# Patch rows of a depthwise convolution laid out as (row, column) instead of (column, row) on the partitions

**Chip, cores, metric.** One core of a Trainium2 chip. The metric is the device time of one execution in microseconds (us); a run's time is the median of its executions.

## The reference

```python
x0 = x + sum over 3x3 of shifted(x) * dw_pe        # depthwise convolution, 511 x 511 x 192, bf16
h  = layernorm(x0)                                 # over the 192 channels
# windows of 7 x 7 (73 x 73 = 5329 of them), 4 heads of 48:
q, k, v = split(h_windows @ w_qkv)
out = softmax(q k^T / sqrt(48)) v @ w_o
return x0 + out
```

## The kernel before

Windows are taken in 42 blocks of 128. For each block the tile XP holds, for every window, the 9 x 9 patch of x around it: 81 partitions, one for each patch position, and (window, channel) along a partition. The convolution is a matmul for each channel: 81 patch positions against T, an 81 x 49 matrix of that channel's taps. XP has one buffer; it is refilled for the next block as soon as the last convolution matmul of this block has read it, and is wanted again some 87 us later.

```python
for j in range(3):                                    # taps, one column of the 3x3 at a time
    nc.sync.dma_start(out=dwK[9 * j : 9 * j + 3, :], in_=dw_pe[:, j, :])
...
def load_xp(blk):
    for (a, b0, b1, p0) in segments(blk):             # runs of windows in one row of windows: 2 or 3
        nb = b1 - b0
        if a == NWR - 1 and blk > 0:
            nc.gpsimd.memset(XP[0:KP, p0 : p0 + nb, :], 0.0)
        else:
            if b0 == 0:
                nc.gpsimd.memset(XP[0:9, p0 : p0 + 1, :], 0.0)            # L119
            if b1 == NWC:
                nc.gpsimd.memset(XP[64:KP, p0 + nb - 1 : p0 + nb, :], 0.0)  # L121
        ...
        for pc in range(9):                           # patch column
            ...                                       # q, sh, bb0, bb1: which column of which window
            nc.sync.dma_start(                        # L139: nine rows onto nine neighbouring partitions
                out=XP[9 * pc + pr0 : 9 * pc + pr1, p0 + bb0 - b0 : p0 + bb1 - b0, :],
                in_=xr[h0 + pr0 : h0 + pr1, bb0 + sh : bb1 + sh, q, :],
            )
...
def conv_tile(blk, it):
    ...
    nc.tensor.matmul(ps[:, col : col + S], lhsT=XP[0:KP, :, c], rhs=T[0:KP, c, :], ...)   # L282
    nc.vector.tensor_tensor(out=xc[...], in0=ps, in1=xc[...], op=ALU.add)                 # L284
```

The stores (L396, SP queue) write XC, the finished block, in pieces of 16 windows; the loads of the next XC (L108, POOL queue) follow piece by piece, and the convolution of the next block adds into it. L412 and L431 are the q, k and v projections, L453 to L560 the attention, L346 the transposes after the norm, L369 the output projection.

## Time and profile before

| | before |
|---|---|
| time, median of 2 | 5343.16 us (5342.79 to 5343.53) |
| span of the profiled run, mean granted PE clock | 5337.2 us, 0.824 |
| first convolution matmul | 109.8 us |
| XP burst of a block: packets, length | 10,330, 53.5 us (mean of blocks 1 to 40) |
| 40 blocks in the middle | 4976.4 us |

The burst lengths and the block times are not a view of the profile: I grouped the XP packets (384 B each) in the trace's packet records, and took a block from the first convolution matmul of one block to that of the next. The profile's wait lines read "who waited, for whom: us in total, times, longest". "issue" as the releaser means that the engine waited for nothing that the profile shows.

### The profile page before, as it was taken

What the parts mean: (1) busy time and instruction counts of PE and PEld (TensorE: products, weight loads), DVE (VectorE), ACT (ScalarE), POOL (GpSimd) and SP (SyncE); (2) the same over time, 40 slices, a digit from 0 to 9 for tenths busy, and PEclk for the clock granted to TensorE, in tenths of its full rate; (3) what the DMA queues carried; (4) which work ended last, traced back from release to release, by engine and by line L of the source; (5) the groups of instructions that cost most, each with busy time, mean ns of one, the idle gap of its engine ahead of it and who ended that gap; (6) DMA issues with size and microseconds to landing.
All of it is one profiled execution on the core that took longest, in us unless ns stands there. A gap on an engine that the chain in (4) does not pass through costs nothing.

```text
span 5337.2 us, 148265 instructions
## 1 busy us (share of the span) xinstructions
PE 4490.1 (84%) x65427; PEld 3661.5 (69%) x65427; DVE 3816.7 (72%) x6912; ACT 2744.5 (51%) x3385; POOL 758.0 (14%) x833
## 2 busy tenths in 40 slices
PE   2788888888888888888988888888888888888887
PEld 1666676667776676677776777767666776677776
DVE  6776777767776777777677777777777777767776
ACT  1554555545555555555555455555555555545555
POOL 1111111111111111111111111111111111111120
PEclk9887888887778887888788877788888888877888
DMA  6554445554455555554455544455555445544431
GB/s 67 51 75 70 68 71 80 82 73 68 68 68 70 71 72 74 71 74 71 68 73 91 75 68 68 68 72 72 74 72 72 73 70 78 85 74 67 68 48 32
DMA packets 512613, 375.27 MB, mean 70 GB/s; under 512 B 453129, under 2 KB 453321, under 8 KB 511958
## 3 DMA queue, kind: packets, MB, share of 16 engines
q1 hardware_dynamic: 480918, 265.08, 38.1%
q0 software_dynamic: 30592, 100.32, 10.6%
q8 instruction: 514, 8.42, 0.7%
q14 instruction: 141, 1.16, 0.1%
q10 hardware_dynamic: 448, 0.30, 0.0%
HBM read 265.31 MB, written 100.27 MB: 68 GB/s over the span
## 4 chain that ended last, share of the span: by engine, by line
PE 44%; DVE 16%; ACT 14%; DMA 12%; SPq 9%; issue 4%; POOL 1%; DVEq 0%; ACTq 0%; POOLq 0%
PE ps L412 12%; PE ps L282 8%; SPq L396 7%; DMA out_dram<-XC 7%; PE ps L369 6%; DMA XC<-in_x_dram 5%; PE ps L453 5%; PE ps L532 4%; DVE kT L424 4%; ACT hT L355 4%; DVE Qb L422 3%; PE ps L431 2%; DVE XC L284 2%; PE ps L560 2%; ACT kT L426 2%
## 5 line engine op out<-in xcount | busy, mean ns | idle before, releaser
L412 PE MATMUL ps<-hT,Wqk 96*128 96x392 bf16 x5336 | 1233.5, 380 | 76.7 <-DVE XC L284 62.2
L478 ACT ACTIVATE PT<-ps 128x784 bf16<-128x784 f32 x667 | 552.7, 829 | 1095.3 <-PE ps L453 1080.3
L421 ACT CAST Qb<-ps 64x784 bf16<-64x784 f32 x667 | 555.3, 833 | 657.5 <-PE ps L412 655.7
L412 PEld LDWEIGHTS <-Wqk 96*128 96x128 bf16 x5336 | 529.4, 108 | 486.1 <-issue 252.5
L284 DVE TENSOR_TENSOR XC<-ps,XC 128x980 bf16<-128x980 f32 x378 | 437.9, 1176 | 503.0 <-PE ps L282 247.2
L282 PE MATMUL ps<-T,XP 81*128 81x49 bf16 x8064 | 744.0, 264 | 55.5 <-DMA XP<-in_x_dram 55.5
L567 ACT CAST OT<-ps 96x784 bf16<-96x784 f32 x667 | 541.0, 811 | 456.0 <-PE ps L560 452.4
L282 PEld LDWEIGHTS <-XP 81*128 81x128 bf16 x8064 | 733.9, 220 | 57.6 <-issue 55.5
L431 PE MATMUL ps<-Wv,hT 96*128 96x192 bf16 x5336 | 663.5, 277 | 16.4 <-DVE On L544 9.0
L532 PE MATMUL ps<-V,PT 49*64 49x49 bf16 x21344 | 542.5, 195 | 159.1 <-DVE Qb L422 81.2
L431 PEld LDWEIGHTS <-hT 96*128 96x128 bf16 x5336 | 548.8, 111 | 180.0 <-issue 91.6
L544 DVE TENSOR_TENSOR On<-ps,rs 128x768 bf16<-128x768 f32 x667 | 634.6, 951 | 16.0
L532 PEld LDWEIGHTS <-PT 49*64 49x64 bf16 x21344 | 466.2, 116 | 260.4 <-issue 217.7
L327 POOL TENSOR_TENSOR D<-ident,rstd 128x896 bf16<-128x896 bf16 x294 | 486.2, 1681 | 1074.8 <-DVE rstd L320 1053.3
L424 DVE CAST kT<-ps 128x784 bf16<-128x784 f32 x462 | 450.0, 974 | 219.2 <-PE ps L412 209.1
L304 DVE BATCH_NORM_STATS2 bnst<-XC 128x6 f32<-128x192 bf16 x2058 | 600.5, 343 | 0.2
L453 PE MATMUL ps<-Qb,kT 128*64 128x98 bf16 x10672 | 408.0, 225 | 180.7 <-DVE Qb L422 132.2
L422 DVE CAST Qb<-ps 64x784 bf16<-64x784 f32 x462 | 451.6, 978 | 110.6 <-ACT Qb L421 100.1
L355 ACT CAST hT<-ps 96x896 bf16<-96x896 f32 x462 | 452.4, 1109 | 135.9 <-PE ps L346 134.9
L560 PE MATMUL ps<-ident,On 128*96 128x98 bf16 x5336 | 412.1, 226 | 114.4 <-DVE kT L424 110.9
L453 PEld LDWEIGHTS <-kT 128*64 128x64 bf16 x10672 | 341.5, 121 | 231.5 <-issue 131.7
L108 POOL DMA_DIRECT2D XC<-in_x_dram x386 | 216.0, 560 | 1865.9 <-DVE rs L543 996.3
(73 smaller groups left out, 4396.2 us busy)
## 6 DMA issues: line engine op xcount, KB each, us to landing
XC<-in_x_dram POOLq DMA_DIRECT2D x277, 294.0 KB, 7.5
out_dram<-XC SPq DMA_DIRECT2D x277, 294.0 KB
XP<-in_x_dram SPq DMA_DIRECT2D x210, 246.4 KB
XP<-in_x_dram SPq DMA_DIRECT2D x68, 243.0 KB
XC<-in_x_dram POOLq DMA_DIRECT2D x37, 165.4 KB, 7.1
out_dram<-XC SPq DMA_DIRECT2D x37, 165.4 KB
XP<-in_x_dram SPq DMA_DIRECT2D x22, 216.0 KB
XP<-in_x_dram SPq DMA_DIRECT2D x18, 212.6 KB
```

The costliest lines, as they stand in the source:

```text
L282: nc.tensor.matmul(ps[:, col : col + S], lhsT=XP[0:KP, :, c], rhs=T[0:KP, c, :], start=True, stop=True)
L304: nc.vector.bn_stats(out=bnst[:, s, :], in_=xc[:, s, :])
L355: nc.scalar.copy(out=hv[0:KT, kt, :, s0 : s0 + NDG], in_=src)
L412: nc.tensor.matmul(ps[:, ab * 512 : ab * 512 + TOK], lhsT=Wqk[kt][0:KT, which * 2 + ab, :], rhs=hT[0:KT, kt, ck * CH : (ck + 1) * CH, 0:S] ...
L421: nc.scalar.copy(out=dst[0:64, :, :, 0, :], in_=src[0:64])
L422: (nc.vector.tensor_copy if dve_help else nc.scalar.copy)(out=dst[64:128, :, :, 1, :], in_=src[64:128])
L424: nc.vector.tensor_copy(out=dst[:, :, 0:TOK], in_=two_bank(ps, TOK))
L431: nc.tensor.matmul(ps[:, col : col + C], lhsT=hT[0:KT, kt, ck * CH + 2 * jj : ck * CH + 2 * jj + 2, :].rearrange("p w s -> p (w s)"), rhs= ...
L453: nc.tensor.matmul(ps[64 * wp : 64 * wp + 64, col : col + 2 * S], lhsT=k_[:, ab, w * S : w * S + 64], rhs=q_[:, ab, w, :, :].rearrange("p ...
L478: nc.scalar.activation(out=pt[:, 0 : 16 * S].rearrange("p (b n) -> p b n", b=2), in_=two_bank(ps, 8 * S), func=ACTF.Exp, scale=scale,)
L532: nc.tensor.matmul(ps[64 * wp : 64 * wp + 64, col : col + S], lhsT=pt[64 * wp : 64 * wp + S, pc_ : pc_ + 64], rhs=v_[64 * wp : 64 * wp + S ...
L544: nc.vector.tensor_tensor(out=o_[:].rearrange("p (b j) (h d) -> p b (j h) d", b=2, d=DH), in0=ov[:, :, :, 0:DH], in1=r_[:].rearrange("p (b ...
```

## The change

The intent: the nine rows of one load should fall on partitions nine apart instead of on nine neighbours. That neighbours slow a load down was the author's assumption. The partition of a patch position becomes 9 x row + column. The taps and the selection pattern that builds T are transposed to match. The halo columns now lie nine partitions apart; the change loads them from a small zero tile where the kernel before used a memset.

```diff
-        nc.sync.dma_start(out=dwK[9 * j : 9 * j + 3, :], in_=dw_pe[:, j, :])
+        nc.sync.dma_start(out=dwK[9 * j : 9 * j + 3, :], in_=dw_pe[j])
...
+    zero = consts.tile([16, C], BF, name="zero")
+    nc.vector.memset(zero[:], 0.0)
+    XPr = XP[0:KP].rearrange("(r q) n c -> q r n c", q=9)
...
             if a == NWR - 1 and blk > 0:
-                nc.gpsimd.memset(XP[0:KP, p0 : p0 + nb, :], 0.0)
-            else:
-                if b0 == 0:
-                    nc.gpsimd.memset(XP[0:9, p0 : p0 + 1, :], 0.0)
-                if b1 == NWC:
-                    nc.gpsimd.memset(XP[64:KP, p0 + nb - 1 : p0 + nb, :], 0.0)
+                nc.gpsimd.memset(XP[64:KP, p0 : p0 + nb, :], 0.0)
+            if a == 0 and blk > 0:
+                nc.gpsimd.memset(XP[0:9, p0 : p0 + nb, :], 0.0)
...
+            if b0 == 0 and blk > 0:
+                nc.sync.dma_start(out=XPr[0, :, p0, :], in_=zero[0:9, :])
+            if b1 == NWC and blk > 0:
+                nc.sync.dma_start(out=XPr[8, :, p0 + nb - 1, :], in_=zero[0:9, :])
...
-                    out=XP[9 * pc + pr0 : 9 * pc + pr1, p0 + bb0 - b0 : p0 + bb1 - b0, :],
+                    out=XPr[pc, pr0:pr1, p0 + bb0 - b0 : p0 + bb1 - b0, :],
...
-        pattern=[[-1, WS], [-9, WS], [1, KP]],
+        pattern=[[-9, WS], [-1, WS], [1, KP]],
```

## The prediction

The sum came to 11 us, 7 from part 2 and 4 from part 5; part 1 counts 0. The 300 packets per us in part 2 are the author's estimate: the nearest rate in the trace of the kernel before is 290, in a block's tail (rival (a)).

> **What bounds the kernel now.** I read the head of the page first, then the chain that ended last, then the waits, then the timeline of one block, then the issue queue that carries the changed loads.
>
> The page: busy shares, DMA queues and chain.
>
> ```profile
> span 5337.2 us, 148265 instructions
> PE 4490.1 (84%) x65427; PEld 3661.5 (69%) x65427; DVE 3816.7 (72%) x6912; ACT 2744.5 (51%) x3385; POOL 758.0 (14%) x833
> ...
> q1 hardware_dynamic: 480918, 265.08, 38.1%
> q0 software_dynamic: 30592, 100.32, 10.6%
> ...
> PE 44%; DVE 16%; ACT 14%; DMA 12%; SPq 9%; issue 4%; POOL 1%; DVEq 0%; ACTq 0%; POOLq 0%
> PE ps L412 12%; PE ps L282 8%; SPq L396 7%; DMA out_dram<-XC 7%; PE ps L369 6%; DMA XC<-in_x_dram 5%; PE ps L453 5%; PE ps L532 4%; DVE kT L424 4%; ACT hT L355 4%; DVE Qb L422 3%; PE ps L431 2%; DVE XC L284 2%; PE ps L560 2%; ACT kT L426 2%
> ```
>
> PE is the densest engine and has the largest part of the chain. The DMA in the chain is the stores (out_dram from XC) and the loads of XC that follow them; the loads of XP, which the change touches, do not appear among the chain's lines, although they are most of queue q1's 480,918 packets. So: busy queue, not the path.
>
> The waits, all engines, the lines that touch XP, XC and the POOL queue:
>
> ```profile
> POOL XP L121 <- PE ps L282: 1525.0, 41, 70.7
> ...
> POOL XC L108 <- DMA out_dram<-XC: 499.1, 248, 33.1
> ...
> DVE XC L284 <- DMA XC<-in_x_dram: 215.9, 34, 10.5
> ...
> PE ps L282 <- DMA XP<-in_x_dram: 55.5, 1, 55.5
> ```
>
> The convolution (L282) waits for XP once in the whole run: at the start. In the other 41 blocks it never does. The 1525 us are POOL waiting to zero the halo of XP until PE has read the old block; POOL is 14% busy and its next work (D from rstd) comes later anyway, so this large number costs nothing by itself. The XC wait of DVE (216 us, 34 times) is the chain proj, store, load, conv; XP is not in it.
>
> One block in the timeline of the SP queue (start, us, instruction):
>
> ```profile
> 2100.62 50.49 SPq L139 DMA_DIRECT2D XP<-in_x_dram  x27
> 2171.47 14.76 SPq L396 DMA_DIRECT2D out_dram<-XC  x10
> ```
>
> Two stretches of the prologue with nothing else running (length, busy time of PE, weight load, DVE, ACT, POOL, then granted clock, DMA share, GB/s):
>
> ```profile
> 85.00:90.00 5.00, 0.00 (x0) 0.00 (x0) 0.00 (x0) 0.00 (x0) 0.00 (x0) 1.00 0.68 71
> 90.00:105.00 15.00, 0.00 (x0) 0.00 (x0) 0.00 (x0) 0.00 (x0) 0.00 (x0) 1.00 0.70 96
> ```
>
> The 27 XP loads of a block are issued in 50 us and done before the stores. From 85 to 105 us every engine is idle and only XP moves, at 71 to 96 GB/s: the prologue is the one place where XP sets the time.
>
> From the trace's packet records I counted the XP packets (384 B) of each block: about 10,330, in 53.5 us on average (44 to 62), so 193 per us or 74 GB/s. From the last packet to the next convolution 25 to 46 us pass (median 33), to the first store 3 us at the least and 11 in the median. Blocks repeat every 124 us.
>
> [...]
>
> [...]
>
> [...]from 40 to 45 us, XC packets (nearly all 5,376 B) start at 25 per us over 16 engines and XP packets at 11 per us[...].
>
> **The change part by part.** The instruction streams, with line and buffer numbers taken out, are identical on PE and ACT. The rest:
>
> 1. XP loads: same count, same 384 B rows, same sources. Only the partition step of the destination goes from 1 to 9. [...]On the path: none of it, as 25 us of slack exist already. Gain per block 0.
>
> 2. Prologue: the first convolution starts at 109.7 us, after 9,686 XP packets. Until about 80 us XP is held back by the XC loads[...]. After it some 5,200 packets go at 185 to 250 per us in 26 us. At 300 per us they take 17, so 9 us gained; in the mixed stretch perhaps 5 more or nothing. Taking half for the doubt about the cause: 7 us.
>
> 3. The 144 small POOL memsets of the halo (72 of 0.25 us at L119, 72 at L121) go; 143 loads from a zero tile come on the SP queue, nine packets each. The single-window loads of before (9 x 384 B too) took 0.3 us to issue, so about 3.5 x 0.3 = 1 us per block on SP[...]. On the path: 0, with the 3 us least distance to the stores as the margin. POOL loses 144 x 0.25 = 36 us of work and the 1525 us of waiting, also off the path.
>
> 4. The last block's halo memset, 11.8 us on POOL, goes from 81 partitions to 17 with the same row length; same time, long before use. T is built with a swapped pattern of the same size, plus one small memset on DVE (16 x 96 words): under 0.3 us.
>
> 5. Instruction fetches share the DMA engines: 1.27 us a fetch on q8 inside XP bursts, 1.15 outside. PE gaps over 2.5 us with an XP burst running, after the prologue, are five and sum to 20 us; two of them (5.7 and 5.8 us) are fetches. A shorter burst may save some 4 us, an unsure item.
>
> Sum: 7 + 4, so about 11 us off. 5343 - 11 = 5332.
>
> **The rivals.** (a) Nothing but noise: the XP rate is set by the cost of a 384 B packet[...]. For it: 249 packets per us held steady from 90 to 105 us, with nothing else running[...]. Against it: in blocks the same loads run at 140 to 200 per us and 290 in the tail, so something shared does bind. Time 5340 to 5346.
>
> (b) [...]faster XP pays: it would have to be through XC loads and stores meeting less traffic. The profile speaks against it, since XP is finished before the first store in every block. It would need 2.5 us in each of the 42 blocks to reach 2%. Time 5240 to 5290.
>
> (c) The strided destination is slower[...]. [...]124 - 21 us (store to end of burst) leaves about 53 + 33 = 86 us for a burst, so XP may slow by 1.6 times before PE waits; at twice the time the cost is about 20 us per block, 850 us, time 6200.[...]
>
> (d) The granted clock. It dips to 0.50 in stretches where PE was fully busy (2070 to 2100 us) and averages 0.824; any saved stall may partly come back as a lower clock.[...]
>
> **Range and chances.** The point is 5332. Below, the mixed part of the prologue could give 20 us and the fetches 10: 5305. Above, no gain plus 0.15% of run difference and a few us of zero loads: 5352. Faster by over 2% (below 5236) would need (b): 3%. Slower by over 2% needs (c): 3%. The rest is the same.
>
> **What would show each step right or wrong.** Step 1: XP bursts per block shorter than 53.5 us[...] or equal (rival a), with PE still waiting for XP only once. Step 2: the single wait of L282 for XP falls from 55.5 us to around 48. Step 3: no L121 wait on POOL, SP's store issues still starting when DVE ends, POOL's wait for rstd growing by what the halo wait gave up. If L282 waits for XP some forty times, or the XP bursts exceed 86 us, I am wrong by (c); if the XC wait of DVE falls well below 216 us, by (b).

## The result and the profile after

The changed kernel takes 5281.6 us (5281.08 to 5282.13, 2 runs): ratio 0.988, 95% interval 0.9851 to 0.9908. A ratio here is the mean time of one kernel's fast runs over that of the other's of the same rounds, so not quite the ratio of the medians. It is 61.6 us less, outside the range of the prediction (5305 to 5352).

| | before | after |
|---|---|---|
| time | 5343.16 us | 5281.6 us |
| first convolution matmul | 109.8 us | 90.4 us |
| XP burst of a block | 53.5 us | 30.7 us |
| packet rate in the burst | 193 per us | 338 per us |
| mean time of an XP packet in a block | 45 to 67 ns | 24 to 25 ns |
| 40 blocks in the middle | 4976.4 us | 4936.8 us |
| mean granted clock of the profiled run | 0.824 | 0.83 |

The span of the profile is 56.8 us shorter: 19.4 us of it are gone by the first convolution, 39.6 in the 40 blocks, and the rest (block 0 and the tail) takes 2.2 us more.

The page after; compare busy shares, queue q1 and the chain:

```profile
span 5280.4 us, 148194 instructions
PE 4450.8 (84%) x65427; PEld 3644.3 (69%) x65427; DVE 3829.8 (73%) x6913; ACT 2740.0 (52%) x3385; POOL 721.8 (14%) x689
...
q1 hardware_dynamic: 483492, 265.58, 21.7%
...
PE 41%; DVE 18%; ACT 15%; DMA 12%; SPq 9%; issue 3%; POOL 1%; DVEq 0%; POOLq 0%; ACTq 0%
```

Queue q1 carries the same bytes (265.58 MB, 265.08 before) in 21.7% of the engines' time instead of 38.1%. PE is busy for 39 us less with the same 65,427 matmuls: that is not a shorter wait, so the clock is the first suspect.

The waits after, the lines that answer to those of the prediction:

```profile
POOL D L331 <- DVE rstd L324: 2552.9, 83, 92.5
...
POOL XC L108 <- DMA out_dram<-XC: 490.7, 241, 33.3
...
DVE XC L288 <- DMA XC<-in_x_dram: 213.6, 32, 8.9
...
PE ps L286 <- DMA XP<-in_x_dram: 36.0, 1, 36.0
```

POOL's 1525 us of waiting for PE have moved into its wait for rstd (1053 before, 2553 now), as predicted. The wait of DVE for XC is what it was. The convolution still waits for XP once, 36.0 us instead of 55.5.

The later part of one block's XP loads in the SP queue with the stores after it (start, us, instruction), and the last stretch of the prologue (columns as in the prediction):

```profile
2079.75 13.08 SPq L144 DMA_DIRECT2D XP<-in_x_dram  x9
2092.88 2.40 SPq L127 DMA_DIRECT2D XP<-zero  x1
2095.33 7.23 SPq L144 DMA_DIRECT2D XP<-in_x_dram  x9
2135.31 14.57 SPq L400 DMA_DIRECT2D out_dram<-XC  x10
```

```profile
80.00:85.00 5.00, 0.00 (x0) 0.00 (x0) 0.00 (x0) 0.00 (x0) 0.00 (x0) 1.00 0.66 139
85.00:89.00 4.00, 0.00 (x0) 0.00 (x0) 0.00 (x0) 0.00 (x0) 0.00 (x0) 1.00 0.64 160
```

With no engine busy, XP moves at 139 to 160 GB/s (the last XC packets still run until 82 us; in the second line XP is alone), where it moved at 71 to 96 before. So the order of the destination partitions limited these loads; by what means inside the chip is not shown.

**Where the 40 us of the blocks come from.** Since PE never waited for XP there, I looked for what else had changed for PE. Waits of PE for instructions, kernel before, five of seven lines:

```profile
PE ps L532 <- issue: 10.2, 6, 2.0
PE ps L431 <- issue: 7.0, 3, 5.6
PE ps L412 <- issue: 5.2, 1, 5.2
PE ps L346 <- issue: 4.3, 3, 2.6
PE ps L560 <- issue: 2.5, 2, 1.9
```

With the two smaller lines (2.3 and 0.9 us) they come to 32.4 us in 18 waits. After the change the same view has no such line among its longest. The longest but one of the waits before, in the timeline of the weight loads:

```profile
489.67 0.14 PEld L412 LDWEIGHTS <-Wqk 96*128 96x128 bf16 x2
495.46 0.13 PEld L412 LDWEIGHTS <-Wqk 96*128 96x128 bf16 x2 [5.65 <-issue]
```

PE stops in the middle of eight equal matmuls for 5.65 us, and the profile shows no operand that it waits for. An XP burst is running (151 packets per us), and in the gap lies a packet of queue q8, an instruction fetch of 16 KB, from 491.9 to 493.5 us. What follows, in stretches of 5 us of the same kernel (the seventh number is the granted clock):

```profile
484.00:489.00 5.00, 4.28 (x91) 3.35 (x93) 4.57 (x16) 4.95 (x7) 0.00 (x0) 1.00 0.76 64
490.00:495.00 5.00, 0.22 (x2) 0.00 (x0) 3.94 (x18) 0.83 (x2) 0.00 (x0) 0.87 0.74 62
495.00:500.00 5.00, 4.53 (x50) 3.03 (x52) 0.00 (x0) 3.25 (x4) 0.00 (x0) 0.50 0.74 75
500.00:505.00 5.00, 5.00 (x41) 3.32 (x38) 4.09 (x19) 3.57 (x5) 0.92 (x1) 0.50 0.74 76
```

These waits are waits for instructions. Numbered in order of time in the packed trace, PE has some 131,200 instructions (matmuls, weight loads, control); queue q8 has 514 packets, so about one for every 256. All 18 waits come at numbers that leave the same remainder, 194, when divided by 256. At all such places the last q8 packet had ended 6.9 us before PE went on (median); at the 18 waits only 1.5 to 2.1 us. So PE stops where the instructions of one fetch end and the next has come late.

The clock falls to 0.50 in the gap and stays there until 510.8 us, 17.1 us in all. This block took 10.1 us longer than the same block after the change, though the wait was 5.65. In this trace 88 of the 89 stretches of half clock last a multiple of 3.4 us, and extra drops of 3.4 to 10.2 us begin beside six more of the 18 waits, which are gaps of 1.2 to 2.0 us. What makes the clock fall and rise again is not shown.

In the 40 blocks the time at half clock falls from 1821 to 1744 us. Half of the difference, 38.6 us, is what the lower clock costs if all work slows in proportion (an estimate from these two times), so in this pair of profiles the clock alone can account for the gain. Eight of the 18 waits have a stretch of half clock that begins beside them, 68 us together. From 47 to 64 us after a block's first convolution, where ten of the 18 waits lie, the time at half clock falls from 87 to 9 us over the 40 blocks; before that it is the same (1596 and 1599 us).

PE's idle time is equal (665 and 663 us): the 32.4 us of waits for instructions went, and three other waits of PE grew by 33.6 us (for hT by DVE, for XC by DVE, for Qb by ACT). That split is one pair's: in another pair below idle time and clock share it. Nor does every microsecond come this way: the 15 of the 40 blocks with such a wait gained 26.9 us, the other 25 gained 12.7, of which 11.9 in one block whose clock stayed low for 71.7 us without a late fetch.

### The profile page after: what moved, and what is told of

Its sections match the earlier page's. It is cut to its first block, busy times and chain, and to the rows that moved or that the text cites. A ratio compares the mean times of both kernels' runs of the same rounds, so it can differ in the third digit from the quotient of the medians.

```text
span 5280.4 us, 148194 instructions
## 1 busy us (share of the span) xinstructions
PE 4450.8 (84%) x65427; PEld 3644.3 (69%) x65427; DVE 3829.8 (73%) x6913; ACT 2740.0 (52%) x3385; POOL 721.8 (14%) x689
## 3 DMA queue, kind: packets, MB, share of 16 engines
q1 hardware_dynamic: 483492, 265.58, 21.7%
## 4 chain that ended last, share of the span: by engine, by line
PE 41%; DVE 18%; ACT 15%; DMA 12%; SPq 9%; issue 3%; POOL 1%; DVEq 0%; POOLq 0%; ACTq 0%
PE ps L416 11%; PE ps L286 8%; SPq L400 8%; DMA out_dram<-XC 7%; PE ps L373 7%; DMA XC<-in_x_dram 5%; PE ps L457 4%; DVE kT L428 4%; PE ps L536 4%; ACT hT L359 4%; DVE Qb L426 3%; DVE XC L288 2%; ACT kT L430 2%; PE ps L435 2%; ACT Qb L426 2%
## 5 line engine op out<-in xcount | busy, mean ns | idle before, releaser
L416 PE MATMUL ps<-hT,Wqk 96*128 96x392 bf16 x5336 | 1207.8, 374 | 82.0 <-DVE XC L288 71.0
L286 PEld LDWEIGHTS <-XP 81*128 81x128 bf16 x8064 | 732.4, 220 | 38.1 <-DMA XP<-in_x_dram 36.0
L350 PE MATMUL ps<-D,XC 128*96 128x128 bf16 x4116 | 350.2, 246 | 168.3 <-DVE hT L361 93.2
```

Source lines behind the costliest of these rows:

```text
L416: nc.tensor.matmul(ps[:, ab * 512 : ab * 512 + TOK], lhsT=Wqk[kt][0:KT, which * 2 + ab, :], rhs=hT[0:KT, kt, ck * CH : (ck + 1) * CH, 0:S] ...
```

## The experiments

Theory 1: loads onto nine neighbouring partitions, called crowded below, are slow; that makes XP bursts long (53.5 us before, 30.7 after), which the prologue pays directly, and it makes PE's instruction fetches late beside a burst (37 of 219 over 1.6 us before, none after), which the blocks pay in gaps (32.4 us) and in clock drops beside them (17.1 us at half clock at the longest gap traced above). Theory 2: the POOL memsets and POOL's wait for PE cost the time. Theory 3: not the crowding but the length of the burst, or the amount of traffic beside PE, costs it. A fourth possibility is chance in the granted clock. All runs below had five timed rounds beside the kernel before on the same chip; the medians of the kernel before were 5346.7, 5342.4 and 5349.9 us in the three sets, its single executions 5322 to 5389 us. Against that scatter the times of two runs in the result look closer together than they are.

**The halo alone, in the old order.** Edit to the kernel before:

```diff
-            else:
+            elif blk > 0:
                 if b0 == 0:
-                    nc.gpsimd.memset(XP[0:9, p0 : p0 + 1, :], 0.0)
+                    nc.sync.dma_start(out=XP[0:9, p0, :], in_=zero[0:9, :])      # same for the right edge
```

> The kernel before (nine neighbouring partitions per load), with the halo zeroed by loads from a zero tile instead of POOL memsets, as the changed kernel does. Theory 1 ([...]XP bursts are slow, the prologue waits for them, and PE's instruction fetches come late beside them, after which the clock is halved for a while): nothing of that changes, so 5335 to 5352 us, ratio 0.998 to 1.002, XP bursts near 53 us. Theory 2 (POOL's memsets and its wait for PE cost the time): most of the gain after the prologue, about 40 us, appears here: 5300 us, ratio 0.992.

Measured: 5348.33 us, ratio 0.9996 (0.997 to 1.0021). First convolution at 112.3 us, bursts 53.8 us, PE waits for instructions 33.8 us in 17 waits. Theory 2 falls from this side: the part of the change that frees POOL is worth nothing.

**POOL's memsets put back into the new order.** Edit to the changed kernel:

```diff
+            if blk > 0 and 0 < a < NWR - 1:      # overwritten by the loads that follow
+                nc.gpsimd.memset(XP[0:9, p0 : p0 + 1, :], 0.0)
+                nc.gpsimd.memset(XP[64:KP, p0 + nb - 1 : p0 + nb, :], 0.0)
```

> The changed kernel with two POOL memsets put back ahead of each segment's loads (on XP, overwritten by the loads that follow), so that POOL waits for PE as before and the loads wait for POOL. Theory 1: bursts stay near 31 us and the time near 5282 us, 5275 to 5292. Theory 2: some 40 us come back, 5320 us.

Measured: 5286.55 us, ratio 0.9887 (0.9866 to 0.9907). POOL waits 1505 us for PE again, bursts 30.6 us, no wait of PE for instructions. Theory 2 falls from the other side too.

**Extra traffic, first attempt.** The changed kernel with five more loads per segment into spare partitions:

```diff
+    XPs = XP[82:127].rearrange("(r q) n c -> q r n c", q=5)    # spread; crowded: "(q r) n c -> q r n c"
...
+                if blk > 0 and 2 <= pc < 7:
+                    nc.sync.dma_start(out=XPs[pc - 2, pr0:pr1, ...], in_=...)    # same source as the load before it
```

> The changed kernel, from block 1 on with five more XP-like loads per segment into partitions that nobody reads (82 to 126), each writing partitions five apart: 56% more packets[...]. Theory 1, in which the crowding and not the amount of traffic or the length of the burst delays PE's fetches: bursts of about 48 to 52 us, as long as before the change, and yet the time within 10 us of the changed kernel, 5275 to 5295, no drop of the granted clock 45 to 65 us after a block's first convolution. Theory 3 (any XP traffic of that length at that moment disturbs PE): about 40 us come back, 5310 to 5330.

> As the run with extra spread loads, but the five extra loads write nine neighbouring partitions each[...]. Theory 1: slower bursts than with spread extras (31 + 5/9 of 53 = about 60 us), late PE fetches and extra clock drops come back in some blocks: 15 to 45 us over the changed kernel, 5297 to 5327. Theory 3: the same as the run with spread extras or a little more.

Measured: 5559.03 us (ratio 1.0395) and 5603.23 us (1.0481), far from every expectation. Both are my mistake. Nothing read the spare partitions, so the scheduler was free to issue the first extras early. The SP queue of the run with spread extras:

```profile
2386.49 13.97 SPq L406 DMA_DIRECT2D out_dram<-XC  x9
2400.51 4.01 SPq L150 DMA_DIRECT2D XP<-in_x_dram  x3
```

Three XP-like loads stand right behind the stores, where the XC loads of the next block are under way. XC lands 14.5 us later in a block (median, counted from its first convolution), and a block takes 7.0 us longer than in the changed kernel. The pair decides nothing between the theories. It shows that such traffic costs 7 us a block when it runs beside the stores and XC loads.

**Extra traffic, held back.** The same two kernels, in which one matmul of the last convolution tile also reads the spare partitions (T is zero there), so that the extras wait for PE as the real loads do; PE's instruction order is unchanged:

```diff
+    nc.vector.memset(T[64:128, C - 1, :], 0.0)
...
+                kp = 127 if c == C - 1 else KP
-                nc.tensor.matmul(..., lhsT=XP[0:KP, :, c], rhs=T[0:KP, c, :], ...)
+                nc.tensor.matmul(..., lhsT=XP[0:kp, :, c], rhs=T[0:kp, c, :], ...)
```

> The extra spread loads again, mended: in the earlier pair the scheduler issued some of the extra loads beside the stores and XC loads, as nothing held them back. Now the last convolution matmul of a block also reads the spare partitions (its T rows there are zero), so that the extras wait for PE as the real loads do. Theory 1: bursts of 45 to 52 us, as long as before the change; PE's fetches inside them at most as slow as in the changed kernel (1.1 to 1.2 us mean) and no clock drops 45 to 65 us after a block's first convolution: 5275 to 5300 us. Theory 3 (length or amount of traffic, not crowding): 5315 to 5345.

> As the run with held spread loads, with the five extras on nine neighbouring partitions each. Theory 1: bursts near 57 us, late fetches and clock drops come back in some blocks, 10 to 45 us over the run with held spread loads. Theory 3: equal to it within 10 us.

Measured: spread 5286.38 us (ratio 0.9888, 0.9853 to 0.9923), crowded 5314.07 us (0.9944, 0.9909 to 0.998). With spread extras the bursts last 49.9 us and carry about half as many packets again, nearly as long as before the change, and the gain is untouched; PE waits 0.8 us for instructions. Theory 3 falls. The crowded run lands in the range that theory 1 gave it, but mostly by another way. PE's wait for the convolution's sums, crowded:

```profile
PE ps L424 <- DVE XC L296: 103.5, 36, 8.9
```

and spread:

```profile
PE ps L424 <- DVE XC L296: 68.0, 35, 7.4
```

The crowded bursts last 62.8 us and end about 2 us before the first store (median; 12.5 with spread extras); the stores start 1 to 2 us later and XC with them. This wait alone grew by 35.5 us, more than the 28 us between the two medians, and waits for instructions are 3.6 us only. So this run shows that crowding lengthens a burst until it meets the stores; it does not show the cost of late fetches: 14 took over 1.6 us (table below), and PE waited twice.

**No XP loads after block 0, old order** (wrong result):

```diff
+                if blk > 0:
+                    continue
                 nc.sync.dma_start(out=XP[9 * pc + pr0 ...
```

> The kernel before with the XP loads left out from block 1 on (wrong result on purpose): no XP traffic after the prologue. Theory 1: the 19 us of the prologue stay lost, the rest of the gain appears at once or a little more, so 5285 to 5310 us, first convolution at 110 us. If the gain after the prologue has nothing to do with XP traffic (theory 2 or chance in the clock): 5335 to 5350.

Measured: 5317.36 us, ratio 0.9952 (0.9917 to 0.9986), between the two expectations. The built program shows why it can't be read cleanly: without the loads the scheduler ordered PE's instructions differently (3,008 of its 65,427 matmuls stand in another place in the trace). Its 40 blocks took 4944 us, 32 less than before, but not with the same program. Inconclusive as a time; but with no XP traffic PE waits only 1.8 us for instructions, in the old order too.

**One half of the change at a time.** The changed kernel, whose loads spread in one part only; the data then don't fit T, which the comparison with the reference does not notice, as the convolution term is small. (So that comparison can't vouch for the new layout either; T's pattern and the loads, both by 9 x row + column, must agree by construction.) Sizes and dependencies are the same, and the instruction order is identical on all five engines:

```diff
-    XPr = XP[0:KP].rearrange("(r q) n c -> q r n c", q=9)
+    XPs = XP[0:KP].rearrange("(r q) n c -> q r n c", q=9)
+    XPn = XP[0:KP].rearrange("(q r) n c -> q r n c", q=9)
...
+        XPr = XPs if blk == 0 else XPn        # the other run: XPs if blk > 0 else XPn
```

> The changed kernel with its instruction streams untouched on every engine; only the destination of the XP loads differs by block: spread (nine apart) for block 0, nine neighbours from block 1 on. Wrong result on purpose. Theory 1 (prologue gains about 20 us, the blocks about 40 by less crowding beside PE's instruction fetches): first convolution near 90 us, later bursts near 54 us, PE waiting for instructions again (some 30 us in all), 5315 to 5333 us. If the gain after the prologue is not from the spread: 5278 to 5292.

> The reverse: nine neighbours for block 0, spread from block 1 on. Wrong result on purpose. Theory 1: first convolution near 110 us, bursts near 31 us, no PE wait for instructions, 5293 to 5310 us. If the gain after the prologue is not from the spread: 5335 to 5350.

Measured:

| spread in | time | ratio (95%) | first convolution | 40 blocks | burst | waits for instructions |
|---|---|---|---|---|---|---|
| block 0 only | 5335.75 us | 0.9968 (0.9947 to 0.9988) | 91.0 us | 4969.5 us | 53.9 us | 35.9 us, 18 times |
| blocks from 1 on | 5307.53 us | 0.9924 (0.9907 to 0.9941) | 111.5 us | 4933.5 us | 30.7 us | none |

Waits of PE, spread in block 0 only:

```profile
PE ps L288 <- DMA XP<-in_x_dram: 36.6, 1, 36.6
PE ps L437 <- issue: 11.5, 3, 6.0
PE ps L538 <- issue: 7.3, 8, 1.7
PE ps L418 <- issue: 7.2, 2, 5.9
PE ps L566 <- issue: 5.4, 2, 3.3
```

Spread from block 1 on:

```profile
PE ps L288 <- DMA XP<-in_x_dram: 57.1, 1, 57.1
```

This is the run that settles it. With the same program, only the destination partitions of the later loads bring the waits for instructions back or take them away, and the gain with them. By the medians the first half is worth 14 us and the second 42 against 5349.9 us; their sum, 56, agrees with the whole within the intervals. The 5335.75 us lie 3 us above the range that I gave it. The profile of that run is of one of its two quickest executions (5317.33 us; the other four took 5334 to 5341), so the profiles of the pair lie closer than the medians. All its 18 waits stand at the same place of every 256 instructions as before the change. Between 47 and 64 us after a block's first convolution the clock is at half for 47 us over the 40 blocks, against 7 in the other run. In this pair the blocks' 36 us divide into 19 of PE idle time and 25 of clock, less 8 of other terms.

Counting the fetches of queue q8 (16 KB each) in the packet records, those that took over 1.6 us beside an XP burst:

| kernel | fetches beside XP | over 1.6 us |
|---|---|---|
| before | 219 | 37 |
| old order, halo by loads | 215 | 34 |
| spread in block 0 only | 219 | 31 |
| new order, held crowded extras | 258 | 14 |
| after | 121 | 0 |
| new order, POOL memsets | 126 | 0 |
| new order, held spread extras | 195 | 0 |
| spread from block 1 on | 119 | 0 |

Away from XP all eight have 17 to 30 such fetches. What is not shown is the path inside the chip on which a crowded load holds a fetch up: the trace names neither the engine of a packet nor the time at which a fetch was asked for.

**A later start.** The changed kernel with the memset of XP done three times, so that the loads start 20.6 us later:

```diff
     nc.vector.memset(XP[:], 0.0)
+    nc.vector.memset(XP[:], 0.0)
+    nc.vector.memset(XP[:], 0.0)
```

> The changed kernel with the memset of XP on DVE done three times, so that everything starts 20.6 us later. If what comes after the prologue does not depend on its phase, the shift shows one to one: 5297 to 5312 us. If the granted clock or the fetches depend on the phase of the kernel's start, the time moves by something else than 20 us (rival: chance in the clock).

Measured: 5297.4 us (5283.82 to 5315.62), ratio 0.9897 (0.9878 to 0.9917). The median is in the range. The way is not quite as expected: in the profile the first convolution comes at 82.3 us, earlier than without the delay, and block 0 takes 99.4 us instead of 82.3, so that block 1 starts 9 us later, not 20.6. The profiled execution was the slowest of the six; its 40 blocks took 4961 us, 24 more than the changed kernel's, with 1835 us at half clock (1744 there) and no late fetch beside XP. The executions scatter over 32 us, so chance in the clock is real at the size of some 15 us either way, and a single pair of profiles can't tell it from an effect of 20 us; it is too small for the 60 us, and the medians of the variants with spread loads agree.

**Larger pieces of XC.** The XC loads and stores have pieces of 16 windows, on 16 neighbouring partitions. The changed kernel with pieces of up to 64:

```diff
-            for o in range(0, b1 - b0, 16):
-                nb = min(16, b1 - b0 - o)
+            for o, nb in chunks(b1 - b0):     # nb = min(64, (n - o) // 16 * 16) or n - o
```

> The changed kernel with XC loads and stores cut at 64 windows instead of 16 (rest as multiples of 16): [...]fewer issues stand in the chain of store and load. Theory 1 carried over: the store and XC stretch of each block (from first store issue to XC landed, 28 us) shortens by 5 us or more in 41 blocks, of which PE sees a part: 5180 to 5270. If pipelining of store and load by 16 windows was worth more[...]: 5290 or slower.

Measured: 5299.54 us, ratio 0.9919 (0.9883 to 0.9954), by the medians slower than the changed kernel (the intervals of the two ratios overlap). The prologue gains 25 us (first convolution 65.4), block 0 gives back 8.5, and the 40 blocks lose 40 (4976.5). In a block the first XC load is issued 4.7 us later and XC lands 1.6 us later: by the kernel's order a load of a piece must wait for the whole store of that piece (POOL waits for stores 241 times in the changed kernel, 490.7 us in all). PE also waits 15.8 us for instructions, in 10 waits, none beside an XP burst and all with XC loads or stores under way: late fetches are not a matter of XP alone. That the larger pieces pipeline worse is my reading of these times, not tested by itself.

**Large pieces in block 0 alone.** The prologue's gain without the blocks' loss:

```diff
+            cuts = [0, (b1 - b0) // 16 * 16, b1 - b0] if blk == 0 else [*range(0, b1 - b0, 16), b1 - b0]
-            for o in range(0, b1 - b0, 16):
-                nb = min(16, b1 - b0 - o)
+            for o, o1 in zip(cuts, cuts[1:]):
+                nb = o1 - o
```

> The changed kernel with block 0's XC loads alone cut in large pieces (64 and 9, 48 and 7 windows), as in the run with 64 everywhere, whose first convolution came 25 us earlier and whose block 0 took 8.5 us longer. If that gain is additive: 16 us under the changed kernel, 5260 to 5272 us, faster than both kernels.

Measured: 5283.36 us (5261.65 to 5289.14), ratio 0.9868 (0.9847 to 0.9889). The first convolution comes at 66.9 us, block 0 takes 88.9, so block 1 starts 16.8 us earlier than in the changed kernel, and the profiled span is 5260.3 us, 20 less. But two executions took 5262 us and the other four 5283 to 5289, and no rounds have it beside the changed kernel. It beats the kernel before; whether it beats the changed one is open.

## Why the prediction was wrong

- **What bounds the kernel.** Right: chain and XC waits hardly changed with XP, and PE waited for XP once, before and after.
- **Part 1, partition order or packet cost.** The partition order did bind: bursts of 30.7 us instead of 53.5, and 24 to 25 ns a packet instead of 45 to 67, with the same 384 B rows. Rival (a), by which the cost of a packet sets the rate, is wrong. The author's reason why neighbours are slow is shown by no run; it is cut, and with it the burst length that part 1 forecast.
- **The failed step: "On the path: none of it ... Gain per block 0."** Spread from block 1 on is worth some 40 us, 1 us a block. The step asked only whether PE waits for the data of a burst. It did not ask what else uses the DMA engines during the burst and stands on PE's path: PE's own instructions (queue q8, 514 packets of 16 KB, 0.7% of the engines' time).
- **Part 5 had the right place and the wrong size.** It allowed "some 4 us". It counted gaps over 2.5 us and compared mean fetch times (1.27 and 1.15 us). The sum of PE's waits for instructions in the waits view was 32.4 us, mostly in gaps under 2.5 us; of its five gaps three were fetches, not two. And the tail of the fetches, not their mean, tells the kernels apart (37 of 219 over 1.6 us, then none).
- **Rival (b) had the number but not the way.** The 5281.6 us lie in its 5240 to 5290; but it wanted the gain from XC, and DVE's wait for XC stayed (215.9 and 213.6 us).
- **Rival (d) had the clock the wrong way round.** It took the clock for something that gives saved stalls back. At the gap of 5.65 us the clock was at half for 17.1 us; in the profile without such gaps the mean clock is 0.83 instead of 0.824.
- **Part 2, the prologue.** Term mis-sized: 7 us predicted, 19.4 measured. It expected at most 5 us from the mixed stretch before 80 us (20 at the low end of its range, which covers this term). By then the changed kernel had moved 6,420 of the 9,686 packets and the kernel before 3,570; at the old rate of 249 per us the difference is 11 us. The remaining tail then runs at 139 to 160 GB/s. That the crowding hurts more while XC loads run too fits these rates, but was not tried by itself.
- **Parts 3 and 4.** Right: the halo by loads in the old order gives 0.9996, POOL's memsets in the new order take nothing (0.9887). The last block's memset took 11.8 us on 17 partitions as on 81, that of the zero tile 0.14 us. The zero loads cost SP 3.4 us a block, not 1, off the path as it said.
- **Smaller slips.** After 80 us 6,116 packets were left, not some 5,200, and from 80 to 85 us they went at 160 per us. The sum "124 - 21" does not give the 86 us of rival (c), which 53 + 33 does. Of the XC packets of the prologue a quarter were of 2,688 B.

## What to carry to other kernels

Ask of a transfer off the critical path not only whether its data come in time, but whom it delays. Here PE's instruction fetches went over the DMA queues too (q8, 514 packets of 16 KB), and with crowded loads in the blocks PE waited 32 to 36 us for instructions in three kernels (before, halo by loads, spread in block 0 only), without a wait in the profile that names the load. Look for "issue" waits of PE inside DMA bursts, add them up, and count the clock drop beside each (17.1 us at half clock at the gap of 5.65 us). When data may lie in any order on the partitions, try another partition step for the rows of one load and measure it (here step 9 against 1: bursts of 30.7 us against 53.5), but do not enlarge the pieces of a store and load chain without measuring: here 64 windows were no better than 16 (ratios 0.9919 and 0.988).
